# Attention scores in 64x32 array tiles with doubled, half-empty states, and another order of the pieces

## The chip, the cores and the metric

The kernel runs on one core of one Trainium2 chip. The metric is the device time of one execution in microseconds (us); the median of three runs counts. A profile is one execution of its own; its times are read against that execution. Engines are called as the profile calls them: PE (matrix engine; PEld is its weight load), DVE (vector), ACT (scalar), POOL (GpSimd), SP (which only issues stores here).

## What is computed

Two steps follow each other: a two-way attention between 512 tokens and 32 states in each of 8 batches and 8 heads, and a dense layer pair over all 4352 rows that come out of it.

```python
def _attn_ref(x, state):              # x (8, 8, 512, 64), state (8, 8, 32, 64)
    scores = scale * np.matmul(x, state.transpose(0, 1, 3, 2))
    ...                               # softmax over the 32 states
    xread = np.matmul(a, state)
    scores2 = scale * np.matmul(state, x.transpose(0, 1, 3, 2))
    ...                               # softmax over the 512 tokens
    sread = np.matmul(a2, x)
    return np.concatenate([xread, sread], axis=2)

def _moe_ref(x, w_in, w_out, s, b):   # d_model 512, d_ff 2048
    r = np.maximum(x @ w_in, 0.0)
    return (s * (r * r) + b) @ w_out
```

## The kernel before, in words

**Pieces and order.** All work is cut into some 700 small pieces, and the list `ORDER` (lines 15 to 76) names them one after the other. A word such as `M.2.3.0` calls one helper (table at lines 712 to 722) with its arguments; a last letter A, V or G says whether ACT, DVE or POOL does it. The list is the order of the instructions *on each engine*: an engine works through its own words in this order and waits only for data and for buffers, so the place of a DVE word between two PE words sets no time by itself. The same holds for DMA issues: loads `x`, `xn`, `win`, `wout` and `st` are issued by POOL and stand in line with POOL's arithmetic, stores by SP (some late ones by ACT).

**Pieces of one batch b** (heads are held as two groups g of four, r is the head in its group):
- `xT` (line 284): DVE transposes 32x32 blocks of x, two 16-bit values e = 0, 1 as a pair. `pair` (253) does the same for the states into `stE`, for the batches of rows i0 to i1.
- `T` (292): scores of all 8 heads against the states, 16 matmuls: for both e, for four output strips hp of 32 rows and both groups g. Weights are a 32x32 block of `stE`, the array tile is (32 r, 32 hp), and the sum over e is made in PSUM (bank g). `keep` copies scores to SBUF for later.
- `U`, `mu`, `D`, `E1`, `z`, `At`, `A` (313 to 359): softmax over the states; `A` is what the dense layer takes. `nm`, `nms`, `E2`, `a2` (364 to 390): softmax over the tokens. `aps`, `a2T` (392, 398) turn it, `V` (401) multiplies it with x, `srd` (421) puts the result away.
- `M` (424): states times one quarter j of w_in, 8 matmuls in array tiles of 64x32, one output strip hp and group g each; `Mc` copies to fp16. So attention's second product and the first dense layer become one: `l` (476) makes 128 rows f of the hidden layer out of `M` and `A` with two matmuls; its ReLU is on ACT (463). `lh` and `sh` are the halves of that for batch 0, `s` (471) squares.
- `L` (499) and `out`: second dense layer for batches 0 to 2. `wsum`, `S`, `P`, `ev`, `put` (530 to 611): the same for batches 3 to 7 with 7 products in place of 8, which needs sums of weights and of activations; a batch has 14 words `P` of 8 matmuls each. `lsr`, `ssr`, `S_sr`, `P_sr`, `ev_sr`: both layers for the state rows, at the end.
- `idle.n` (666): n matmuls on ones, at the start.

**Buffers in PSUM.** `ps_t` and `ps_a` hold one tile of two banks each, and `T`, `M`, `V`, `aps` and others take turns in them (third argument of `M`, second of `T`: 1 is `ps_t`). `ps_h` holds two tiles for `l`, `ps_o` two for `L` and `P`.

**Head and strip.** In `T`, `V` and `M` the strip hp of a head r in group g is r ^ g (lines 298, 409, 429):

```python
r = hp ^ g
mm(part(T[Ns * hp : Ns * hp + Ns], p, g)[:, 0, :],
   stE[32 * r : 32 * r + 32, NG * b + g, :, e],
   part(at[b]["xT"][32 * r : 32 * r + 32, :, :, e], p, g)[:, 0, :],
   ..., tp=(32 * r, Ns * hp))
```

Of the kernel before, what the change touches and what calls it, by code (L numbers as in the profile page):

```python
# [10 lines left out]
FP32 = mybir.dt.float32  # L11
FP16 = mybir.dt.float16
# [12 lines left out]
    "bias",  # L25
# [54 lines left out]
def kernel(  # L80
# [12 lines left out]
    nc = tc.nc  # L93
    AF = mybir.ActivationFunctionType
    ALU = mybir.AluOpType
    AX = mybir.AxisListType

    B, H, S, D = x.shape
    Ns = state.shape[2]
    DM = H * D  # L100
    DF = moe_w_in.shape[1]
    P = 128
    NK = DM // P
    NKF = DF // P
    NG = H // 4
# [55 lines left out]
    stE = konst.tile([P, NR, Ns, 2], FP16, name="stE")  # L161
# [61 lines left out]
    nc.vector.memset(ones32, 1.0)  # L223
    xh_t[0] = xpool.tile([P, NG, NT, D], FP16, name="xh_0", tag="xh")
# [28 lines left out]
    def pair_states(i0, i1):  # L253
        nc.vector.transpose(
            stE[:, i0:i1].rearrange("p i n e -> p (i n e)").bitcast(FP32),
            stn[:, i0:i1].rearrange("p i d -> p (i d)").bitcast(FP32),
        )

# [33 lines left out]
    def at_T(b, own=1, p=None):  # L292

        at[b]["T", p] = T = two_banks(f"T_{b}_{p}", own=own)
        for e in range(2):
            for hp in range(4):
                for g in range(NG):
                    r = hp ^ g
                    mm(
                        part(T[Ns * hp : Ns * hp + Ns], p, g)[:, 0, :],  # L300
                        stE[32 * r : 32 * r + 32, NG * b + g, :, e],
                        part(at[b]["xT"][32 * r : 32 * r + 32, :, :, e], p, g)[:, 0, :],
                        start=(e == 0), stop=(e == 1),
                        tp=(32 * r, Ns * hp),
                    )
# [451 lines left out]
```

## Time and profile before

| What | Value |
|---|---|
| Median of three runs (lowest, highest) | 218.31 us (218.29, 219.01) |
| The profiled execution's own time | 218.81 us |
| Its span, first to last instruction | 217.0 us |
| PE, PEld busy | 207.7 us, 126.5 us |
| DVE, ACT, POOL busy | 169.8 us, 155.2 us, 103.8 us |
| Granted TensorE clock, mean over the span | 1.000 |
| DMA moved | 22.68 MB |

A matmul's duration in the profile reaches from its first column to the end of its writing, so two in a row overlap and their durations add up to more than the time they take. What a row of matmuls takes is read from start to start. A busy share of 96% says that PE nearly always has a matmul under way, not that it streams at its best.

### The profile page before, as it was taken

How to read it: one execution, taken by the hardware profiler on the slowest of the kernel's cores; microseconds unless marked ns; L12 is line 12 of the kernel's file. 1: busy time of each engine (PE TensorE's matmuls, PEld its weight loads, DVE VectorE, ACT ScalarE, POOL GpSimd, SP SyncE). 2: the span in 40 equal slices, each digit the busy share in tenths (PEclk: the TensorE clock that was granted, in tenths of full speed). 3: DMA queues.
4: the chain of work that ended last, by engine and by line, in shares of the span. 5: the costliest groups of instructions: out<-in, count | busy, mean ns of one | idle time of the engine just before them, and what ended most of it. 6: DMA issues, size and time to landing. Idle time of an engine off the chain costs nothing.

```text
span 217.0 us, 4732 instructions
## 1 busy us (share of the span) xinstructions
PE 207.7 (96%) x1920; PEld 126.5 (58%) x1920; DVE 169.8 (78%) x237; ACT 155.2 (72%) x263; POOL 103.8 (48%) x100
## 2 busy tenths in 40 slices
PE   7868999999999999999999999999999999999992
PEld 2334344343444435545677666776667777888881
DVE  2789885989867869985998799979887964785472
ACT  4477987898858678989889899677669766454400
POOL 8229033494579930434254318837455334225330
PEclk9999999999999999999999999999999999999999
DMA  6999992659597252192908850719912600440045
GB/s 149 236 204 202 205 197 40 103 136 127 118 172 125 48 97 51 24 167 55 145 7 134 133 119 3 98 30 146 200 17 59 139 0 3 91 106 0 0 145 148
DMA packets 23657, 22.68 MB, mean 105 GB/s; under 512 B 4436, under 2 KB 17236, under 8 KB 23636
## 3 DMA queue, kind: packets, MB, share of 16 engines
q0 software_dynamic: 16560, 12.26, 39.4%
q1 hardware_dynamic: 5792, 9.18, 17.2%
q10 hardware_dynamic: 1284, 0.95, 1.6%
q8 instruction: 15, 0.25, 0.4%
q14 instruction: 6, 0.05, 0.1%
HBM read 25.72 MB, written 8.91 MB: 160 GB/s over the span
## 4 chain that ended last, share of the span: by engine, by line
PE 88%; DMA 6%; POOL 2%; ACT 1%; issue 0%; DVE 0%; ACTq 0%; POOLq 0%
PE hps L459 24%; PE ops L503 19%; PE opf_X L138 16%; PE opf_W L138 8%; DMA w_out<-in_moe_w_out_dram 6%; PE opf_Y L138 4%; PE mps L138 4%; PE hps_sr L459 3%; PE vps L138 2%; PE aps L138 2%; PE ops_sr_X L138 2%; PE T_None L138 2%; POOL w_in L201 1%; PE ops_sr_W L138 1%; PE hph L138 1%; POOL xh L184 1%
## 5 line engine op out<-in xcount | busy, mean ns | idle before, releaser
L463 ACT ACTIVATE r<-hps 128x512 f16<-128x512 f32 x120 | 67.5, 602 | 27.8 <-PE hps L459 27.0
L459 PE MATMUL hps<-A,M 128*128 128x512 f16 x240 | 64.8, 380 | 0.0
L138 PEld LDWEIGHTS <-g 128*128 128x128 f16 x480 | 46.6, 98 | 11.4 <-issue 0.7
L503 PE MATMUL ops<-w_out,g 128*128 128x512 f16 x192 | 46.3, 379 | 0.2 <-DMA w_out<-in_moe_w_out_dram 0.2
L469 POOL TENSOR_TENSOR g<-r 128x1024 f16<-128x1024 f16 (+1 forms) x14 | 30.4, 2182 | 24.3 <-ACT r L463 24.3
L459 PEld LDWEIGHTS <-M 128*128 128x128 f16 x240 | 21.7, 98 | 22.8 <-issue 6.4
L503 PEld LDWEIGHTS <-g 128*128 128x128 f16 x192 | 18.7, 98 | 22.5 <-issue 0.8
L153 ACT CAST M<-mps 128x1024 f16<-128x1024 f32 x22 | 22.3, 1017 | 1.6 <-PE mps L138 1.6
L467 ACT ACTIVATE g<-r 128x1024 f16<-128x1024 f16 (+1 forms) x18 | 21.4, 1210 | 0.1
L193 POOL DMA_DIRECT2D xn<-in_x_dram x32 | 18.6, 595 | 5.7 <-PE vps L138 4.9
L344 POOL TENSOR_TENSOR At<-E,rz 128x1024 f16<-128x1024 f16 x5 | 9.8, 1964 | 22.0 <-ACT r L463 11.4
L138 PE MATMUL opf_X<-w_T,g 128*128 128x256 f16 x160 | 19.8, 273 | 0.0
L573 DVE TENSOR_TENSOR g<-g 128x1024 f16<-128x1024 f16 (+1 forms) x20 | 17.9, 908 | 1.1 <-POOL S L573 0.9
L573 POOL TENSOR_TENSOR g<-g 128x1024 f16<-128x1024 f16 x4 | 8.8, 2206 | 19.6 <-PE opf_X L138 12.4
L469 DVE TENSOR_TENSOR g<-r 128x1024 f16<-128x1024 f16 (+1 forms) x18 | 14.7, 837 | 1.6 <-ACT r L463 1.6
L153 DVE CAST M<-mps 128x1024 f16<-128x1024 f32 x10 | 12.1, 1213 | 3.6 <-PE mps L138 3.0
L602 DVE SCALAR_TENSOR_TENSOR osx<-opf_X,sb_bc,bias_bc 128x512 f32<-128x512 f32 x15 | 11.2, 747 | 4.0 <-PE opf_X L138 3.9
L290 DVE STREAM_TRANSPOSE xT<-xh 128x1024 f32<-128x1024 f32 (+2 forms) x12 | 10.4, 874 | 4.4 <-ACT xh L153 3.9
L323 POOL TENSOR_TENSOR Dm<-U,mu 128x1024 f32<-128x1024 f32 x3 | 5.7, 1912 | 14.8 <-DVE mu L319 14.8
L463 ACT ACTIVATE r_sr<-hps_sr 128x256 f16<-128x256 f32 x16 | 6.1, 381 | 7.9 <-PE hps_sr L459 7.2
L138 PE MATMUL mps<-w_in,stT 64*32 64x512 f16 x256 | 11.3, 383 | 0.5 <-DMA w_in<-in_moe_w_in_dram 0.3
L513 DVE SCALAR_TENSOR_TENSOR osb<-ops,sb_bc,bias_bc 128x512 f32<-128x512 f32 x12 | 8.8, 736 | 3.4 <-PE ops L503 3.4
(101 smaller groups left out, 324.8 us busy)
## 6 DMA issues: line engine op xcount, KB each, us to landing
out_dram<-osx SPq DMA_DIRECT2D x36, 128.0 KB, 2.4
xn<-in_x_dram POOLq DMA_DIRECT2D x32, 128.0 KB, 5.3
xh<-in_x_dram POOLq DMA_DIRECT2D x14, 256.0 KB, 4.8
w_in<-in_moe_w_in_dram POOLq DMA_DIRECT2D x8, 256.0 KB, 9.9
w_out<-in_moe_w_out_dram POOLq DMA_DIRECT2D x4, 512.0 KB, 11.3
out_dram<-osb SPq DMA_DIRECT2D x16, 128.0 KB, 3.3
xf<-in_x_dram SPq DMA_DIRECT2D x4, 256.0 KB, 5.2
out_dram<-osb SPq DMA_DIRECT2D x16, 64.0 KB, 4.4
```

The costliest lines, as they stand in the source:

```text
L138: return nc.tensor.matmul(out, lhsT, rhs, start=start, stop=stop, tile_position=tp, is_transpose=is_transpose, skip_group_check=skip,)
L153: (engine.copy if engine is nc.scalar else engine.tensor_copy)(out, in_)
L193: nc.gpsimd.dma_start(out=xn_t[b][32 * jh : 32 * jh + 32].rearrange("t h c d -> t h (c d)"), in_=x[b].rearrange("h (t jh c) d -> jh t h (c ...
L290: nc.vector.transpose(part(out, p, g), part(in_, p, g))
L344: e.tensor_tensor(out, E1, over_n(rz), ALU.mult)
L459: nc.tensor.matmul(hps, lhsT, rhs, start=(i == 0), stop=(i == len(terms) - 1))
L463: nc.scalar.activation(R_t[tag, q][:, i], hps, AF.Relu)
L467: nc.scalar.activation(g, r, AF.Square)
L469: e.tensor_mul(g, r, r)
L503: nc.tensor.matmul(ops_t[tag, rr], G_t[tag][:, f, P * rr : P * rr + P], w_out_f(f), start=(f == 0), stop=(f == NKF - 1),)
L573: e.tensor_tensor(out, x, y, op)
L602: nc.vector.scalar_tensor_tensor(out, fast(b, name[0]), s_bc, out if plus else bias, ALU.mult, ALU.add)
```

## The change

Three things are changed together.
1. **States are stored twice.** `stE` becomes `stZ[0]` and `stZ[1]`. `pair` transposes as before into `stZ[0]`; then two DVE multiplications by the columns of a mask `own` (1 for the rows of heads of one parity, 0 for the other) leave in `stZ[k]` only heads with r % 2 = k, the other head's 32 rows being zero. `own` is made at the start by five small memsets.
2. **`T` works in tiles of 64 rows.** Each of its 16 matmuls takes the 64 rows of a pair of heads; the wrong head meets zero weights. The array tile is (64 (r // 2), 32 hp). Strip and head are now paired by r = hp ^ 2g in `T`, `V` and `M`; the tile of `M` stays (64 g, 32 hp). Counts, columns and accumulation are as before.
3. **All pieces stand in a new order**, and some change their engine or are cut otherwise (a square of 4 rows in place of two of 2, a sum in halves). The three `idle` words go from 12, 12 and 5 matmuls to 11, 10 and 3. Every other PE word occurs in both lists.

```diff
-    stE = konst.tile([P, NR, Ns, 2], FP16, name="stE")
+    stZ = [konst.tile([P, NR, Ns, 2], FP16, name=f"stZ_{k}") for k in range(2)]
+    own = konst.tile([P, 2], FP32, name="own")
...
     nc.vector.memset(ones32, 1.0)
+    nc.vector.memset(own, 0.0)
+    for r in range(4):
+        nc.vector.memset(own[Ns * r : Ns * r + Ns, r % 2 : r % 2 + 1], 1.0)
...
     def pair_states(i0, i1):
         nc.vector.transpose(
-            stE[:, i0:i1].rearrange("p i n e -> p (i n e)").bitcast(FP32),
+            stZ[0][:, i0:i1].rearrange("p i n e -> p (i n e)").bitcast(FP32),
             stn[:, i0:i1].rearrange("p i d -> p (i d)").bitcast(FP32),
         )
+        for k in (1, 0):
+            nc.vector.tensor_scalar(stZ[k][:, i0:i1], stZ[0][:, i0:i1], own[:, k : k + 1], None, ALU.mult)
...
-                    r = hp ^ g
+                    r = hp ^ 2 * g
+                    rows = slice(64 * (r // 2), 64 * (r // 2) + 64)
                     mm(
                         part(T[Ns * hp : Ns * hp + Ns], p, g)[:, 0, :],
-                        stE[32 * r : 32 * r + 32, NG * b + g, :, e],
-                        part(at[b]["xT"][32 * r : 32 * r + 32, :, :, e], p, g)[:, 0, :],
+                        stZ[r % 2][rows, NG * b + g, :, e],
+                        part(at[b]["xT"][rows, :, :, e], p, g)[:, 0, :],
                         start=(e == 0), stop=(e == 1),
-                        tp=(32 * r, Ns * hp),
+                        tp=(64 * (r // 2), Ns * hp),
                     )
...
-                    hp = k ^ g
+                    hp = k ^ 2 * g
...
-                r = hp ^ g
+                r = hp ^ 2 * g
```

The start of the list, then the stretch around the piece `V.5.2`, then the end:

```diff
-    "castx.1.0.A xT.0.1.0 casts.A idle.12 pair.0.4 castx.0.0.A xT.0.0.0 T.0.1.0 U.0.0 turn.0.4.A mu.0.0 "
-    "D.0.V.0 E1.0.0 sb idle.12 castx.1.1.V keep.0.0 xT.0.1.1 castx.0.1.A win.0 M.1.0.0 M.0.0.1 x.1 z.0.0 "
-    "xT.0.0.1 At.0.V.0 A.0.0 win.1 wout.0 T.0.0.1 U.0.1 Mc.1.0.A mu.0.1 D.0.V.1 Mc.0.0.A lh.0.2.0 xT.1.1 "
-    "lh.0.0.0 keep.0.1 xT.1.0 idle.5 E1.0.1 win.2 M.0.1.0 T.1.1 sh.0.0.0.V Mc.0.1.A z.0.1 At.0.V.1 A.0.1 "
-    "lh.0.6.0 lh.0.4.0 keep.1 sh.0.6.0.V sh.0.4.0.V sh.0.2.0.G L.0.1.0 lh.0.0.1 lh.0.4.1 lh.0.2.1 M.0.2.0 "
-    "Mc.0.2.A lh.0.6.1 L.0.0.0 win.3 l.0.8 l.0.10 M.1.2.1 Mc.1.2.A M.0.3.0 U.1 mu.1 D.1.V l.0.11 "
-    "sh.0.2.1.V wout.1 l.0.9 M.1.1.1 wout.2 Mc.0.3.V wout.3 sh.0.0.1.V M.1.3.0 E1.1 l.0.13 l.0.12 st "
-    "s.0.10.2.V L.0.0.1 L.0.1.1 z.1 Mc.1.3.A x.2 s.0.12.2.A l.0.15 At.1.V s.0.8.2.G L.0.1.2 l.0.14 A.1 "
+    "win.0 win.1 castx.1.0.A xT.0.1.0 x.1 castx.0.0.A casts.A idle.11 xT.0.0.0 turn.0.4.A castx.1.1.A "
+    "wout.0 pair.0.4 T.0.1.0 U.0.0 mu.0.0 D.0.V.0 sb E1.0.0 xT.0.1.1 castx.0.1.A z.0.0 At.0.V.0 xT.0.0.1 "
+    "keep.0.0 idle.10 M.1.0.0 Mc.1.0.A M.0.0.1 Mc.0.0.A A.0.0 T.0.0.1 U.0.1 keep.0.1 mu.0.1 lh.0.2.0 "
+    "lh.0.0.0 D.0.V.1 E1.0.1 xT.1.0 M.0.1.0 idle.3 win.2 xT.1.1 Mc.0.1.A T.1.1 win.3 keep.1 z.0.1 "
+    "At.0.V.1 sh.0.0.0.G sh.0.2.0.G lh.0.4.0 lh.0.6.0 sh.0.4.0.G L.0.1.0 A.0.1 lh.0.2.1 lh.0.4.1 lh.0.0.1 "
+    "M.0.2.1 U.1 wout.1 Mc.0.2.A lh.0.6.1 wout.2 st sh.0.6.0.V L.0.0.0 l.0.8 sh.0.4.1.G l.0.10 M.0.3.1 "
+    "sh.0.2.1.V M.1.2.0 Mc.1.2.A l.0.11 l.0.9 mu.1 D.1.V E1.1 M.1.1.1 sh.0.6.1.G sh.0.0.1.G Mc.0.3.V "
+    "M.1.3.0 l.0.14 L.0.0.1 s.0.10.2.V l.0.15 Mc.1.3.A L.0.1.1 s.0.8.2.V l.0.12 z.1 At.1.V wout.3 "
+    "Mc.1.1.A l.0.13 L.0.0.2 A.1 L.0.1.2 l.1.11 s.0.14.2.V l.1.2 cps.0 cps.1 pair.4.16 cps.2 cps.3 c "
...
+    "nm.6 nms.6.A wsum.T2.1.G ev.3.Y P.3.5 l.4.13 aps.2 xn.2 ev.3.X2 S.3.4.2.G l.4.8 P.3.6 U.6 mu.6 nm.0 "
+    "P.3.8 a2T.2.V wsum.T4.1.G P.3.7 ev.3.W1 E2.6.0 P.3.9 ev.3.X3 E2.6.1 s.4.12.4.A M.6.0.1 s.4.6.2.A "
+    "V.5.2 srd.2 srd.5 a2.6 s.4.4.2.A S.4.3.0.V l.4.10 S.4.1.0.V nms.0.V P.3.10 wsum.T4.0.G P.3.12 P.3.11 "
...
-    "P.7.8 P.7.9 ssr.6.2.A S_sr.3.0.V ssr.14.2.A ssr.10.2.A P_sr.0 ev.7.X3 S_sr.1.2.G P.7.10 S_sr.2.0.V "
-    "S_sr.3.1.V P.7.11 ev_sr.0.0.X.0.0 P.7.12 P.7.13 put.6.1.0 put.6.1.1 ev.7.W2 put.7.0.0 S_sr.2.1.V "
-    "ev.7.X4 P_sr.1 P_sr.2 P_sr.3 ev_sr.0.1.X.0.0 P_sr.4 ev_sr.1.1.W.0.0 put.7.0.1 put.7.1.0 S_sr.4.2.G "
-    "ev_sr.0.0.Y.1.1 put.7.1.1 ev_sr.1.1.X.1.1 P_sr.5 P_sr.6 ev_sr.0.1.W.1.1 ev_sr.1.0.X.0.1",
+    "ev.7.X3 lsr.13 ssr.8.2.V lsr.12 P.7.10 ssr.12.2.V P.7.12 S_sr.1.1.V S_sr.3.2.V S_sr.2.0.V P.7.13 "
+    "ev.7.X4 P_sr.0 P.7.11 put.6.1.0 P_sr.1 ev_sr.0.0.X.0.0 S_sr.4.0.G S_sr.2.1.G P_sr.2 P_sr.3 ev.7.W2 "
+    "ev_sr.0.1.X.0.0 put.6.1.1 put.7.0.0 P_sr.4 S_sr.4.1.G ev_sr.1.1.W.0.0 P_sr.5 put.7.0.1 put.7.1.0 "
+    "put.7.1.1 ev_sr.1.1.X.1.1 P_sr.6 ev_sr.0.0.Y.1.1 ev_sr.0.1.W.1.1 ev_sr.1.0.X.0.1",
```

How the tiled PE words stand side by side (a row of them with no other PE word between is called a cluster here, a part of a cluster in one tile shape a segment; before, `T` and `M` differ in shape, after they don't), from `L.0.1.0` on:

| | clusters | segments | `T` beside `M` in one cluster | `V` beside `M` |
|---|---|---|---|---|
| before | 23 | 29 | T.2/M.2.3, T.3/M.2.0, T.5/M.3.3, T.6/M.5.1 | V.3.4/M.5.0, V.6.0/M.6.3 |
| after | 22 | 25 | none of two shapes; in one shape: T.2/M.2.3, T.3/M.2.0, T.5/M.3.3, T.6/M.5.1, T.7/M.6.1 | V.3.4/M.5.0, V.5.2/M.6.0, V.6.0/M.6.3 |

More of the change, by code (lines that the diff above doesn't have):

```diff
@@ L15 @@
 ORDER = [
[9 rows of a table removed]
-    "bias",
[50 rows of a table removed]
[58 rows of a table added]
 ]
```

89 rows, old and new, of the table ORDER are left out of this document.

## Prediction

> **What bounds the kernel now.** I read the page's busy shares first, then its slices, then the table by stretches of time, then PE's timeline from start to start.
>
> ```profile
> PE 207.7 (96%) x1920; PEld 126.5 (58%) x1920; DVE 169.8 (78%) x237; ACT 155.2 (72%) x263; POOL 103.8 (48%) x100
> ...
> PE   7868999999999999999999999999999999999992
> ```
>
> PE is busy in every slice but those at the two ends. The table by stretches (PE, PEld, DVE, ACT, POOL busy in each) sharpens it:
>
> ```profile
> 60.00:100.00 40.00, 40.00 (x336) 17.83 (x335) 32.11 (x42) 31.98 (x55) 20.86 (x17) 1.00 0.54 93
> 100.00:140.00 40.00, 40.00 (x419) 27.81 (x417) 35.71 (x50) 34.70 (x57) 20.85 (x21) 1.00 0.59 93
> 140.00:180.00 40.00, 40.00 (x405) 28.55 (x405) 32.72 (x48) 29.48 (x52) 19.45 (x16) 1.00 0.46 81
> ```
>
> PE has 40.00 of 40.00 us at full clock, DVE at most 35.7, ACT 34.7. Busy can hide slow rows, so I take steps from PE's timeline:
>
> ```profile
> 18.78 1.02 PE L503 MATMUL ops<-w_out,g 128*128 128x512 f16 x4 [0.22 <-DMA w_out<-in_moe_w_out_dram]
> 19.64 1.04 PE L138 MATMUL hph<-A,M 128*128 128x256 f16 x8
> 20.99 0.60 PE L138 MATMUL hph<-A,M 128*128 128x256 f16 x4 [0.31 <-ACT rh L489]
> ...
> 24.20 0.63 PE L138 MATMUL mps<-w_in,stT 64*32 64x512 f16 x16
> 24.76 1.04 PE L459 MATMUL hps<-A,M 128*128 128x512 f16 x4
> ...
> 37.98 0.60 PE L459 MATMUL hps<-A,M 128*128 128x512 f16 x2
> 38.51 0.64 PE L138 MATMUL T_None<-xT,stE 32*32 32x512 f16 x16
> 39.08 0.41 PE L138 MATMUL mps<-w_in,stT 64*32 64x512 f16 x8
> 39.42 0.60 PE L459 MATMUL hps<-A,M 128*128 128x512 f16 x2
> ```
>
> Four `ops` take 0.86 (18.78 to 19.64), so a word `l` 0.43 and `L` 0.86; elsewhere a word `P` takes 0.87. Two `M` together take 0.56 (24.20 to 24.76), one alone 0.34 (39.08 to 39.42): 0.22 each plus 0.12 once. The two `hps` ahead of `T` take 0.53 instead of 0.43: entering a tiled cluster costs 0.10. `T` takes 0.57 (38.51 to 39.08): 0.45 plus the same 0.12, paid although `M`, tiled too, comes next. So a cluster costs 0.10, and each segment in one tile shape 0.12.
>
> With these steps I add up PE from `L.0.1.0` at 18.78: 120 `l` 51.8, 48 `L` 41.4, 70 `P` 61.1, state rows 13.1, four `lh` 1.7, aps 3.6, `V` 4.1, six `T` 2.7, 29 `M` 6.4, the few others 1.5, 29 segments 3.5, 23 clusters 2.3: 193.2. PE really needs 194.1 (18.78 to 212.8); 0.9 is stall, nearly all before 27 us. From there PE streams to the end, and the tail (212.8 to 217.0) is one eviction and a store. **The bound is PE's own stream from 18.78 on, and 18.78 is when w_out.0 lands.**
>
> **The change, part by part.**
>
> *T in 64x32.* Counts and columns stay. Eight of its matmuls run at once before (16 of 512 columns in 0.45, as 16 of `M` in 64x32 take 0.44), and eight distinct tiles remain, so `T` costs 0.45 after too. Gained are segments: `T` beside `M` no longer changes shape. By the table of clusters, 29 segments become 25 and 23 clusters 22: 4 x 0.12 + 0.10 = **-0.58**. Bounds: 0 if the 0.12 is paid between any two kinds of tiled work, -0.58 if it is the shape's; I take -0.58, since two `M` in a row pay it once.
>
> [...]
>
> *States twice.* `pair` adds two multiplications. The nearest row is DVE's TENSOR_SCALAR of 128x512 f16 by a column, 364 ns. For 128x256 I take 0.2 each (bounds 0.1 to 0.36), for 128x768 0.5 (0.36 to 0.73). The five memsets (the row of 1x128 has 165 ns) make 0.8 in DVE's 3.05 us of waiting for the first xh: hidden. The first `pair` lies ahead of `T.0.1.0` and now behind castx.0.0 as well: `T.0.1.0` about 0.9 later than 6.12. Its chain made A.0.0 ready at 12.6, while `lh.0.2.0` waits for Mc.0.0 until 13.7, because of w_in.0; the cover is 1.1, the cost nothing, 0.2 if both multiplications take the upper bound. The second `pair` falls where DVE stood idle 1.19 and 1.28 us around `c` and `bias`: nothing, and if that cover is gone `T.2.1` waits for xT.2 by up to 1.0.
>
> *Start.* POOL now issues win.1 ahead of x.1; the 2 MB up to w_out.0 are the same, so it lands at 18.8 again. x.1 lands where win.1 did, near 15.9, and xT.1 begins at 15.4 in halves: `T.1.1` perhaps 0.2 later, under the wait for w_out.0 (0.22 of it is left). Likewise the dummies (29 to 24) all lie ahead of that wait: nothing. Both half squares that `L.0.1.0` needs are POOL's now, not one (1.30 each; 0.38 on DVE): from rh.0.0.0 at about 15.8 to 18.4, in time by 0.4. keep.1 now stands ahead of two ReLUs on ACT, and I find `lh.0.0.1` waiting about as long as `lh.0.2.1` did. Stalls there: same, within 0.7.
>
> *The other moves.* Over the whole list, with a duration for each kind from its row, ACT loses 1.3 us, POOL 2.8, and DVE gains 1.5 beside the masks. None becomes the bound over a stretch, so only single deadlines count. Three are tight. (1) `V.5.2`: from P.3.5's end PE has 5.25 until it; DVE needs ev 0.72, U, mu, nm 3 x 1.25 with gaps, a2T.2 0.69, hand-offs 0.2: 5.36, 0.1 late. (2) The end: from lsr.12 to P_sr.2 six words, 5.24; ReLU 0.6, squares and sums on DVE 0.42 + 0.42 + 0.69 + 0.42, two halves on POOL 1.19 each, hand-offs 0.3: 5.23, just in time. (3) P.3.0 needs out.2.3, 0.75 after L.2.3.3, and has 0.95. I allow **+0.15** for all (bounds 0 and 1.0).
>
> *Sum.* -0.58 + 0.15 = -0.43. The profiled execution took 218.81, 217.0 of it span: 216.6 + 1.81 = 218.4 by it. The median shown is 0.50 lower, 218.31, and goes to **217.9**.
>
> **The rivals.**
>
> A, the sum: 217.9, chance 0.56, by itself 217.2 to 218.7.
>
> B, slower: **w_out.1 comes late.** POOL's line shows where it stands before:
>
> ```profile
> 9.94 0.61 POOL L201 DMA_DIRECT2D w_in<-in_moe_w_in_dram  x1 [3.55 <-DMA w_in<-in_moe_w_in_dram]
> 15.03 1.30 POOL L469 TENSOR_TENSOR g<-rh 128x512 f16<-128x512 f16 x1 [4.47 <-ACT rh L489]
> 16.28 1.27 POOL L201 DMA_DIRECT2D w_in<-in_moe_w_in_dram  x2
> 17.54 2.27 POOL L207 DMA_DIRECT2D w_out<-in_moe_w_out_dram  x3
> ```
>
> The ninth load (9.94) waits until the first has landed; after, win.3 follows it at once and waits for the next landings, to about 13, ahead of POOL's squares. w_out.1 was issued at 17.54. After, it stands behind sh.0.4.0.G, which waits for a ReLU at about 19.05: issue at 20.35. `L.0.0.1` wants it at 27.1. The four loads of w_out took 8.6 to 13.8 to land; at 8.6 from the issue it lands at 29.0, and PE stands 1.9: 219.8. It decides from a landing over 6.75 after the issue. Against it: loads land in the order of issue at some 0.5 MB per 2.5 us (w_in.0 11.2, w_out.0 18.8, the states 32.5), and what lies ahead is no more than before, so the bytes, not the issue, set about 26.2. Chance 0.15.
>
> C, the change does not do what it says: the 0.12 stays between `T` and `M`. Only 0.10 for the cluster is left, and V.5.2 beside M.6.0 saves nothing: 218.4. Against it the row of two `M`. Chance 0.10.
>
> D, slower: **two row tiles on one bank.** After, tiles of rows 0 and 64 both write bank g of `T`, in other strips; in `M` each row tile has a bank of its own. Were they to take turns, each of six `T` would take 0.45 more: 220.6. Against it: before, four row tiles (32 r for r = 0 to 3) write one bank, and `T` keeps the pace of `M`. Chance 0.04.
>
> [...]
>
> E, faster: **the stalls of the start go.** 0.9 lies before 27 us, all of it ReLU or `Mc` wait; if the new order of ACT clears 0.7: 217.2. For it: POOL takes four half squares off DVE, and `Mc.1.1` leaves DVE. Against it: the producers ahead of each wait are the same. Chance 0.15.
>
> **How the numbers follow.** A measurement tells about 0.5% from no change: 217.2 and 219.4 are the marks. Faster: most of E (0.11) and A's lower end (0.13): 0.24. Slower: B (0.12), D (0.04), A's upper end, two of the tight deadlines missed at once (0.01): 0.17. Same: 0.59. For the range, A with C and E reach from 216.9 (E with no tight deadline missed) to 218.7, B to 219.8; outside stay D and the ends, under 0.2.
>
> **What would show it.** In PE's timeline: `T` then `M` in one cluster 0.45 + 0.34 from start to start (right), 0.57 + 0.34 (C), 0.9 for `T` (D). The first `ops` at 18.8 and the second group of `ops` for q = 1 near 27, with no wait for w_out (B if there is one). The step sum from `L.0.1.0`: 192.6 and a stall total below 1.2. V.5.2 waiting for DVE a2T, P_sr.2 for POOL: at most 0.2 each. Wrong I would be above all if many small waits of 0.1 to 0.3 stand in the stretches 100 to 180, where DVE is fullest, or if w_out.0 itself lands at another time than 18.8: every 0.1 of that goes straight into the result.

## The result, and the profile after

The changed kernel takes **224.08 us** (median of six executions, 223.11 to 225.94) against 218.30 for the kernel before beside it: a ratio of 1.026, interval 1.0235 to 1.0294. The forecast was 217.9, with 219.8 as its upper end.

The profiled execution took 223.11 us with a span of 221.2. On its page PE's busy line reads much as before (209.1 us, 95%); the slices show where it does not: a 7 and an 8 in the middle of PE's row (about 127 to 138 us), and a 7 in the row of the granted clock.

```profile
PE 209.1 (95%) x1915; PEld 126.0 (57%) x1915; DVE 176.8 (80%) x248; ACT 154.9 (70%) x261; POOL 101.5 (46%) x102
...
PE   7869999999999999999999978999999999999992
...
PEclk9979999999999999999999999999999999999999
```

The table by stretches (PE, PEld, DVE, ACT, POOL busy, then clock, DMA share, GB/s) puts it at 120 to 140. Before, PE had 20.00 there and the DMA engines were 0.54 busy.

```profile
100.00:120.00 20.00, 20.00 (x246) 13.60 (x245) 17.14 (x25) 15.77 (x26) 16.43 (x10) 1.00 0.33 55
120.00:140.00 20.00, 18.16 (x174) 12.71 (x172) 15.18 (x26) 14.40 (x25) 8.14 (x13) 1.00 0.76 133
```

PE's timeline, with the rows that answer to those of before (first column start, second duration):

```profile
18.55 1.03 PE L508 MATMUL ops<-w_out,g 128*128 128x512 f16 x4
19.64 1.05 PE L136 MATMUL hph<-A,M 128*128 128x256 f16 x8
...
27.47 1.02 PE L508 MATMUL ops<-w_out,g 128*128 128x512 f16 x4 [0.26 <-DMA w_out<-in_moe_w_out_dram]
...
39.38 0.65 PE L136 MATMUL T_None<-xT,stZ 64*32 64x512 f16 x16
39.84 0.40 PE L136 MATMUL mps<-w_in,stT 64*32 64x512 f16 x8
40.17 0.61 PE L464 MATMUL hps<-A,M 128*128 128x512 f16 x2
...
130.52 1.04 PE L464 MATMUL hps<-A,M 128*128 128x512 f16 x4
133.40 1.91 PE L136 MATMUL opf_X<-w_T,g 128*128 128x256 f16 x16 [1.84 <-DVE osx L607]
```

`T` then `M` take 0.46 and 0.33 from start to start: the tiles do what was forecast. But `T.2.1` starts at 39.38 and not at 38.51, and at 130.52 four `hps` of 0.86 are followed by the next row only 2.88 later. The row that PE waits for is DVE's `ev.4.X1`, and that one waits for a store:

```profile
128.22 1.22 DVE L578 TENSOR_TENSOR g<-g 128x2048 f16<-128x2048 f16 x1
132.59 0.75 DVE L607 SCALAR_TENSOR_TENSOR osx<-opf_X,sb_bc,bias_bc 128x512 f32<-128x512 f32 x1 [3.15 <-DMA out_dram<-osx]
...
153.70 0.75 DVE L607 SCALAR_TENSOR_TENSOR osx<-opf_X,sb_bc,bias_bc 128x512 f32<-128x512 f32 x1 [1.14 <-DMA out_dram<-osx]
```

`osx` has one buffer for each half of a batch's rows, so `ev.4.X1` may write only when the four stores of this half of batch 3 are done. SP issues them from 123.45 on. Before, the last eviction into this half (`ev.3.W2`) and the `ev.4.X1` that follows stood further apart, and neither waited:

```profile
120.83 0.74 DVE L602 SCALAR_TENSOR_TENSOR osx<-opf_W,sb_bc,osx 128x512 f32<-128x512 f32 x1
...
129.22 0.75 DVE L602 SCALAR_TENSOR_TENSOR osx<-opf_X,sb_bc,bias_bc 128x512 f32<-128x512 f32 x1
```

POOL's timeline of the changed kernel shows what is issued beside the stores, and the DMA view of 118 to 132 what that does (last column: median us from issue to landing):

```profile
120.47 1.16 POOL L183 DMA_DIRECT2D xh<-in_x_dram  x2
121.61 4.04 POOL L192 DMA_DIRECT2D xn<-in_x_dram  x7
125.81 0.58 POOL L192 DMA_DIRECT2D xn<-in_x_dram  x1 [0.15 <-issue]
```

```profile
xn<-in_x_dram POOLq DMA_DIRECT2D x8, 128.0 KB, 7.7
out_dram<-osx SPq DMA_DIRECT2D x8, 128.0 KB, 7.1
```

The same view of the kernel before:

```profile
out_dram<-osx SPq DMA_DIRECT2D x8, 128.0 KB, 2.4
```

`x.7`, `xn.6` and `xn.0` stand one behind the other on POOL in the new list. Before, POOL issued them at 112.4, 116.3 and 134.3.

**The account**, from the start of `L.0.1.0` to the start of `P_sr.6`: 197.55 against 193.17, +4.38. Against the steps that the prediction used, waits ahead of `T.2.1` are 2.04 in place of 0.72 (+1.32), the store wait is 2.02, a second one 0.89 (`ev.5.X1` at 153.70; the sum `S.5.1.1` on POOL comes late through it, `D.7` stands right behind it there, and a DVE sum beside `D.7` takes 2.38; PE stalls at 158.8 to 161.3), two late rows behind `V.7.1` 0.42, and the tiles give -0.58: 4.07 together. The other 0.31 lies in smaller differences, 0.21 of it ahead of `T.2.1`, where the whole difference is 1.53 (20.83 against 19.73, and the old list has one word `l` of 0.43 more there).

### The profile page after: what moved, and what is told of

The parts are those of the page before. It is cut to its first block, busy times and chain, and to the rows that moved or that the text cites. A ratio compares the mean times of both kernels' runs of the same rounds, so it can differ in the third digit from the quotient of the medians.

```text
span 221.2 us, 4735 instructions
## 1 busy us (share of the span) xinstructions
PE 209.1 (95%) x1915; PEld 126.0 (57%) x1915; DVE 176.8 (80%) x248; ACT 154.9 (70%) x261; POOL 101.5 (46%) x102
## 4 chain that ended last, share of the span: by engine, by line
PE 64%; DMA 11%; DVE 9%; ACT 5%; POOL 4%; issue 2%; SPq 2%; DVEq 0%; POOLq 0%
PE ops L508 16%; PE hps L464 16%; PE opf_X L136 10%; DMA out_dram<-osx 5%; PE opf_W L136 4%; DMA w_out<-in_moe_w_out_dram 4%; PE hps_sr L464 3%; PE mps L136 3%; PE opf_Y L136 2%; DVE osx L607 2%; DVE g L578 2%; DMA xf<-in_x_dram 2%; SPq L616 2%; POOL g L474 2%; PE ops_sr_X L136 2%
## 5 line engine op out<-in xcount | busy, mean ns | idle before, releaser
L468 ACT ACTIVATE r<-hps 128x512 f16<-128x512 f32 x120 | 68.4, 605 | 29.4 <-PE hps L464 28.0
L349 POOL TENSOR_TENSOR At<-E,rz 128x1024 f16<-128x1024 f16 x6 | 12.3, 2043 | 36.3 <-DVE rz L340 23.9
L474 DVE TENSOR_TENSOR g<-r 128x1024 f16<-128x1024 f16 (+1 forms) x22 | 20.5, 945 | 7.3 <-ACT r L468 7.3
L472 ACT ACTIVATE g<-r 128x1024 f16<-128x1024 f16 (+1 forms) x18 | 22.7, 1265 | 0.2
L474 POOL TENSOR_TENSOR g<-r 128x1024 f16<-128x1024 f16 (+1 forms) x7 | 14.9, 2139 | 13.6 <-ACT r L468 13.5
L578 DVE TENSOR_TENSOR g<-g 128x1024 f16<-128x1024 f16 (+1 forms) x20 | 19.1, 957 | 0.9 <-POOL g L578 0.5
L578 POOL TENSOR_TENSOR g<-g 128x1024 f16<-128x1024 f16 (+1 forms) x4 | 10.5, 2619 | 14.2 <-DVE S L578 5.5
L151 DVE CAST M<-mps 128x1024 f16<-128x1024 f32 x9 | 10.8, 1212 | 1.0 <-PE mps L136 1.0
L637 POOL TENSOR_TENSOR g_sr<-g_sr 128x512 f16<-128x512 f16 x3 | 3.4, 1155 | 15.8 <-DVE g_sr L637 15.7
L136 PE MATMUL opf_Y<-w_out,g 128*128 128x256 f16 x80 | 10.2, 273 | 0.0
```

The costliest lines, as they stand in the source:

```text
L136: return nc.tensor.matmul(out, lhsT, rhs, start=start, stop=stop, tile_position=tp, is_transpose=is_transpose, skip_group_check=skip,)
L151: (engine.copy if engine is nc.scalar else engine.tensor_copy)(out, in_)
L349: e.tensor_tensor(out, E1, over_n(rz), ALU.mult)
L468: nc.scalar.activation(R_t[tag, q][:, i], hps, AF.Relu)
L472: nc.scalar.activation(g, r, AF.Square)
L474: e.tensor_mul(g, r, r)
```

## The experiments

The theory after these traces: **(S)** the order costs the time, by putting loads beside stores that a single buffer must wait for. Rivals: the doubled states and their masks cost it; the stores are late for another reason; the start costs it; a lower clock costs it.

### The tiles without the order

The changed code with the list of before.

> The changed kernel's code (states twice, T in 64x32) with the order of before. If the order is at fault and the tiles do what the step sum says: 218.3 - 4 x 0.12 us for the shape changes that go (T beside M in four clusters), so 217.8, T then M 0.45 + 0.34 from start to start, no new stall. If the tiles or the doubled states are at fault: near 224.

Measured: 219.17 (ratio 1.0032, 1.0011 to 1.0054). Each `T` beside an `M` is 0.12 shorter, yet the kernel does not gain. DVE's timeline shows the masks (the two multiplications at L263) between `stZ` and `xT`, and PE's the wait:

```profile
36.70 0.57 DVE L258 STREAM_TRANSPOSE stZ<-stn 128x384 f32<-128x384 f32 x1
37.30 0.88 DVE L263 TENSOR_SCALAR stZ<-stZ,own 128x768 f16<-128x768 f16 x2
38.09 1.24 DVE L296 STREAM_TRANSPOSE xT<-xh 128x1024 f32<-128x1024 f32 x1
```

```profile
39.38 0.65 PE L138 MATMUL T_None<-xT,stZ 64*32 64x512 f16 x16 [0.52 <-DVE xT L296]
```

So in PE's steps the masks eat what the tiles save, about 0.5 against 0.5, because of where `pair.4.16` stands. The expected 217.8 was missed by more than that: the median is 0.70 above the kernel before beside it. In the profile 0.29 of this is a later `L.0.1.0` (19.07 against 18.78), and 0.36 lies behind it (193.53 against 193.17).

### The order without the tiles

The code of before with the new list.

> The code of before (32x32, states once) with the new order. If the order is at fault: 224.1 plus the 0.6 that the tiles save, 224 to 225, with the same waits: DVE for a store near 132 and near 153, PE for w_out near 27 and 34. If the tiles are at fault: near 218.

Measured: 224.72 (1.028, 1.024 to 1.032), with `ev.4.X1` waiting 3.17 for the same stores. **The order alone makes the loss**; the masks are out as its cause.

### Two buffers for the first output tile

```diff
-t = opool.tile(..., tag=f"osx{key}", bufs=1)
+t = opool.tile(..., tag=f"osx{key}", bufs=2 - int(key))
```

Room for it comes from one buffer less for `osb` (4 to 3) and one shared by `stf` and `c16`.

> The changed kernel, with a second buffer for output tile 0 of batches 3 to 7 (room for it comes from one buffer less for the outputs of batches 0 to 2 and from letting two small tiles share a place), so that the first eviction of a batch no longer waits for the stores of the one before. If those store waits make up the middle part of the loss: PE's 1.84 before P.4.4 and the 0.54 near 160 go, 224.1 falls by 2.5 to 3.5 to 220.6 to 221.6. If the eviction would be late for another reason (DVE's own backlog): by less than 1.

Measured: 219.75 (1.0046, 1.0027 to 1.0065). Both waits are gone, though the stores still take 6.9 us to land. PE's rows at the place of the first:

```profile
129.10 1.04 PE L464 MATMUL hps<-A,M 128*128 128x512 f16 x4
129.97 1.91 PE L136 MATMUL opf_X<-w_T,g 128*128 128x256 f16 x16
```

**Without the wait, 4.3 of the 5.8 us are gone**, more than the 2.5 to 3.5 that were expected. Not all of it is the wait itself. In the two profiles (223.11 and 218.78) PE's stalls behind the stores make 2.91; another 1.41 lies ahead of `T.2.1` (39.38 against 37.97), where no store is waited for, and where the clock was halved from 13.30 to 16.70 in the one profile and full in the other. That the clock makes this 1.41 is argued, not shown.

### Loads moved away from the stores, with one buffer

First `x.7` alone, to ahead of `S.3.4.2.G`:

> The changed kernel with one load, x.7, moved in POOL's queue to ahead of S.3.4.2 (issued some 10 us sooner), so that only xn.6 and xn.0 are under way when batch 3 is stored. If the loads that share the DMA engines make the stores slow: stores of 128 KB that took 7 us near 125 take 4 to 6, the wait of ev.4.X1 falls from 3.1 to 1 to 2, the time by 1 to 2, to 222 to 223. If the stores are slow by themselves (number, order on their queue): no change.

Measured: 222.35. The stores still took 6.5 us and `ev.4.X1` waited 2.86, so the wait hardly fell: the eight loads of `xn.6` and `xn.0` are enough. That the time came out in the expected 222 to 223 is luck: it fell by 1.73, the wait by 0.29 only. Two of the four executions had a mean clock of 1.00; of the six of the changed kernel none had (0.982 to 0.996). Then these too:

> The changed kernel, still with one buffer for the first output tile, but with its loads of x taken apart: x.7 goes ahead of S.3.4.2.G, xn.6 goes to where V.5.2 gives its buffer free (behind srd.5), and xn.0 goes behind At.6.G. So no load is issued just ahead of the stores of batch 3. Theory (the eight row loads in one go are what makes those stores land in 7 us): the stores land in 2.5 to 4 us, the wait of ev.4.X1 falls from 2.9 (with x.7 moved alone) to below 0.8, PE's stall there from 1.7 to below 0.3, and the time from 222.35 to 220.3 to 221.0, since the second wait (ev.5.X1) and the stalls of the start stay. Rival (the stores are slow because they are issued late and in long runs by SP, whatever the loads do): the wait stays above 2 us and the time at 222.0 to 222.7.

Measured: 223.66 (1.0254, 1.0195 to 1.0313), 2.7 more than the theory allowed, and yet its mechanism is in the trace: the stores land in 2.4 us and no eviction waits for them. The loss is a new wait that this edit made itself. `xn.6` needs a buffer that `V.5.2` frees, and `wsum.T4.0` stands behind it on POOL:

```profile
113.86 2.13 POOL L548 TENSOR_TENSOR w_T<-w_out,w_T 128x1024 f16<-128x1024 f16 x1
118.44 2.35 POOL L192 DMA_DIRECT2D xn<-in_x_dram  x4 [2.45 <-PE vps L136]
120.81 2.13 POOL L548 TENSOR_TENSOR w_T<-w_out,w_T 128x1024 f16<-128x1024 f16 x1
```

```profile
122.99 1.03 PE L136 MATMUL opf_X<-w_T,g 128*128 128x256 f16 x8 [2.93 <-POOL w_T L548]
```

With `xn.6` behind that sum, and `xn.7` taken from the stores of batch 4 as well:

> The changed kernel, still with one buffer for the first output tile, and its loads kept clear of the stores without a new wait on POOL: x.7 ahead of S.3.4.2.G, xn.6 behind wsum.T4.0.G (in the run with xn.6 behind srd.5, POOL stood 2.45 us for V.5.2 there, with wsum.T4.0.G queued behind it, and PE stalled 2.93), xn.0 behind At.6.G, and xn.7 behind S.5.1.1.G, so that it is clear of the stores of batch 4 too. Theory (loads crowd the stores, and this alone makes ev.4.X1 and ev.5.X1 wait): the stores of both batches land in 2.4 to 4 us, each of the two waits is below 0.5, and the time is that of the kernel with two buffers, 219.0 to 220.2. Rival (one buffer is too little even then, because ev.4.X1 comes 6.0 us behind the last eviction of batch 3 instead of 7.6): a wait of 1 us or more stays, and 220.5 to 222.

Measured: 220.97 (1.0102, 1.0067 to 1.0138). Stores of both batches land in 2.4, and no eviction waits for one; the time lies in the range of the rival, but the wait that the rival named is not there. PE stalls 1.37 behind 157.50, a new stall again made by this edit: `D.7` on POOL now stands behind the issues of `xn.7`, and runs from 155.68.

```profile
157.50 1.03 PE L464 MATMUL hps<-A,M 128*128 128x512 f16 x4
159.73 1.91 PE L136 MATMUL opf_W<-w_out,g 128*128 128x256 f16 x16 [1.21 <-DVE osx L607]
```

So `xn.7` goes one word later on POOL (`S.5.1.1`, called a square in what follows, is a sum):

> The kernel with its loads kept clear of the stores and one buffer (220.97 median), with xn.7 one word later on POOL, behind D.7.G instead of ahead of it. In that run D.7 started 2.47 us behind S.5.1.1 and not 0.1, ACT's E1.7 waited 0.73 for it with two ReLUs queued behind, and PE stalled 1.37 at 157.50. Theory (this stall is only the xn.7 issues ahead of D.7; the stores no longer cost anything): no stall there, no wait of ev.4.X1 or ev.5.X1 above 0.3, and 1.1 to 1.5 less, 219.4 to 219.9, which is the time with two buffers (219.75). Rival (the stall at 157.50 is the late square S.5.1.1 on POOL, which stays where it is): 220.6 to 221.2 again.

Measured: **219.76** (1.0044, 1.0023 to 1.0066), the 219.75 of the two buffers; the stall is gone. The way by `E1.7` and the ReLUs on ACT is not the one in the trace, though: PE's row at 159.73 waited for DVE's `ev.5.W1`, which stood behind a sum of 128x2048 that took 2.82 beside `D.7` in the one run; with `xn.7` later it takes 1.22, since `D.7` then runs beside the sum ahead of it (1.80). One buffer is enough: `ev.4.X1` starts 4.8 us behind the end of the last eviction into this half (124.28) and does not wait, since the last of the four stores landed at 128.57; in the changed kernel it stood ready after 6.0 us and waited 3.15 more.

```profile
123.53 0.75 DVE L607 SCALAR_TENSOR_TENSOR osx<-opf_W,sb_bc,osx 128x512 f32<-128x512 f32 x1
...
129.12 0.74 DVE L607 SCALAR_TENSOR_TENSOR osx<-opf_X,sb_bc,bias_bc 128x512 f32<-128x512 f32 x1
```

### The same fault put into the kernel before

Two words of the old list moved, `xn.6` and `xn.0` behind `S.4.3.0.G`:

> The kernel before, with nothing changed but two words of its order: xn.6 and xn.0 both go behind S.4.3.0.G, so that POOL issues their eight row loads in one go from about 122.4, beside the stores of batch 3 (issued from 121.6). Theory: these stores land in 5 to 8 us instead of 2.4; ev.4.X1 comes 7.6 us behind the last eviction of batch 3 there, so it waits 0.3 to 1.7 us for them, and the time rises from 218.4 to 218.7 to 220.0. Rival (the load burst is harmless, the slowness of the stores comes from something else in the new order): 2.4 us to land, no wait, 218.2 to 218.6.

Measured: 219.76 against 218.79 beside it (1.0043, 1.0010 to 1.0076). The stores, which landed in 2.4, now take 5.9, and an eviction that never waited waits (DVE's timeline, then the DMA view of 118 to 132):

```profile
131.14 0.75 DVE L602 SCALAR_TENSOR_TENSOR osx<-opf_X,sb_bc,bias_bc 128x512 f32<-128x512 f32 x1 [1.23 <-DMA out_dram<-osx]
```

```profile
out_dram<-osx SPq DMA_DIRECT2D x8, 128.0 KB, 5.9
xn<-in_x_dram POOLq DMA_DIRECT2D x8, 128.0 KB, 7.1
```

The first two stores, issued ahead of the loads (122.20 and 122.78, the loads from 122.96 on), still landed in 2.4; the next two took 4.9 and 6.9. With the fault taken out of one kernel and put into the other, (S) is shown: loads beside the stores make the wait. How much of the loss is the wait stands under the run with two buffers.

### The start and the clock

What is left with two buffers is 1.3 us. In the changed kernel's profile the clock is halved for 3.4 us, just behind a stretch in which PE was busy for half of the time (columns as in the table by stretches):

```profile
9.90:13.30 3.40, 1.69 (x35) 0.42 (x33) 2.99 (x7) 3.16 (x5) 1.22 (x2) 1.00 1.19 208
...
13.30:16.70 3.40, 3.09 (x26) 1.45 (x19) 3.33 (x6) 2.58 (x6) 0.45 (x1) 0.50 1.20 206
```

Eight `hph` take 1.82 there from start to start (13.64 to 15.46); at 17.67, where the clock is full, 0.88. By an estimate from this stretch (half of 3.4, of 221), one such stretch brings the mean clock of an execution to 0.992. With two buffers 8 of 10 executions were at 0.992 or below; of the kernel before, 2 of 94 beside all these runs. So dummies were put into the gaps of PE (on top of two buffers):

> The changed kernel with two buffers for the first output tile (219.75 median), and with three dummy products more ahead of M.0.0.1 and three ahead of T.0.0.1, where PE stood idle 0.87 and 0.69 us. The dummies compute nothing that is used. Theory (short idle stretches of PE in the first 13 us bring a stretch of half clock of some 3.4 us, which costs about 1 us): the granted clock is 1.0 (0.996 or more) in nearly all executions instead of 0.992 in most, and the median falls by 0.7 to 1.1, to 218.6 to 219.1. Rival (the clock falls for another reason, such as the load of all engines): the clock stays at 0.992 in most executions and the time at 219.5 to 219.9, or up to 0.3 longer if a dummy is in the way.

> The changed kernel with two buffers for the first output tile, two dummies more ahead of M.0.0.1 and three ahead of T.0.0.1, keep.0.0 ahead of castx.0.1 on ACT, and srd.1 behind s.7.8.2 instead of right behind srd.7. Theory (what is left over the step sum is the wait of M.0.0.1 for keep.0.0 and the two reads of the state rows back to back on ACT): 0.3 to 0.5 less than with the dummies alone, since the 0.14 and 0.27 behind V.7.1 go and the start gains up to 0.3: 218.1 to 218.6, about the kernel before. Rival (the start is set by another chain, and the ReLUs are late anyway): the same as with the dummies alone, within 0.2.

Measured: 219.67 and 219.63. The first half of the theory held in part: 4 and 2 of 12 executions are still at 0.992 or below. The second failed: the medians did not fall. Within the first of these runs, executions at 0.992 or below average 220.28 and the others 219.43, 0.85 apart; in the second they are 0.43 apart, with two buffers alone 0.40 (two executions against eight), and in the last run with one buffer 0.16, where the 8 of 12 executions above 0.992 still average 219.60. So in these runs the halved clock is not most of the 1.3 us. In the profile of the first run with dummies `L.0.1.0` starts at 19.37 and not 17.93; in that of the second it starts at 18.04, but PE then waits 0.41 and 0.29 around the second and last load of w_out. Moving `srd.1` did not remove the late rows behind `V.7.1` either (0.39 in one place instead of 0.14 and 0.27). How the 1.3 us divide stays open.

### The tiles with the masks in a gap

The run of the tiles alone, with one word moved:

```diff
-cps.3 Mc.1.1.V l.1.10 s.1.10.2.G l.1.6 L.0.0.3 c bias l.1.0 l.1.5 pair.4.16 xT.2
+cps.3 Mc.1.1.V l.1.10 s.1.10.2.G l.1.6 L.0.0.3 pair.4.16 c bias l.1.0 l.1.5 xT.2
```

> The change of the tiles alone, in the order of before (219.17 median), with pair.4.16 moved from behind bias to ahead of c, where DVE stood idle 1.19 us. Theory (the 0.52 us that T.2.1 waited for xT.2 is the masks' time, and with the masks in that gap the saving of the tiles comes through): T.2.1 waits 0.1 at most, T then M take 0.46 and 0.34, and the time falls by 0.5, to 218.5 to 218.8, with the late start (0.29) as the remainder. Rival (the states land too late, near 34 us, so that pair there holds c up and with it bias and cps): the wait moves to bps and PE keeps 0.4 or more of it: 219.0 to 219.6.

Measured: 218.30 (0.9989, 0.9965 to 1.0013), and once more:

> The tiles of the change in the order of before with pair.4.16 ahead of c, once more, to narrow its interval (218.30 against 218.42, ratio 0.9989 with 0.9965 to 1.0013). Theory (four of the segments of 0.12 go, and nothing else changes from L.0.1.0 on): 0.3 to 0.5 less than before, 217.9 to 218.2. Rival (the masks ahead of T.0.1.0 delay the start by as much in most executions): no difference, 218.3 to 218.6.

Measured: **217.82** against 218.79 (0.9951, 0.9928 to 0.9974). The states had landed in time (`pair` starts at 32.05, right behind `Mc.1.1`; in the first of the two profiles it waited 0.27 for them), `T.2.1` waits for nothing, and from `L.0.1.0` to `P_sr.6` PE needs 192.83 and 192.70 in the two profiles, 0.34 and 0.47 less than before. The gains by the medians, 0.12 and 0.97, lie on both sides of that, and the medians of the kernel before beside them differ by 0.37; the traces bear out 0.3 to 0.5. This version has the lowest median of all here.

## Why the prediction was wrong, point by point

**"None becomes the bound over a stretch, so only single deadlines count. Three are tight"**: this step failed. Only deadlines between arithmetic pieces were searched. `V.5.2`, `P_sr.2` and `P.3.0` held without a stall, but the deadline that mattered was that of a buffer: the stores of batch 3 against `ev.4.X1`. It was not in the list, nor among the rivals, because in the profile of before no eviction waits for a store. The margin was in that profile all the same: the last eviction into this half of batch 3 ended at 121.57, SP issued its four stores one after the other from 121.60 to 123.46, the last of them landed at 125.93, and `ev.4.X1` began at 129.22, 3.3 us later. The new list both cut the time between the two evictions from 7.6 to 6.0 us and put 1.5 MB of loads beside the stores, the last of which landed at 132.47. The term of "+0.15, bounds 0 and 1.0" measured 2.9 in PE's rows; without the wait the median fell by 4.3.

**"Start ... same, within 0.7"**: wrong by about as much again. Stalls between `L.0.1.0` and `T.2.1` are 2.04, not 0.72. In the profile with two buffers, at full clock, `T.2.1` comes 20.04 behind `L.0.1.0` and not 20.83, so 0.79 of the 1.53 does not recur there. That `L.0.1.0` came at 18.55, near the forecast 18.8, is luck: by the trace w_out.0 landed at 17.85, and PE did not wait for it; the rows ahead ran at half clock. With two buffers and full clock `L.0.1.0` came at 17.93.

**Rival B** happened in small: w_out.1 was issued at 20.38 (20.35 was worked out) and PE waited 0.26 for it, not 1.9, so the landing was about 7 us behind the issue and not 8.6. The last load of w_out, which stands behind three half squares, cost another 0.34, and this was not looked at.

**Tiles, -0.58**: right in the steps. In the old list, where four segments go (0.48), the two profiles gave 0.34 and 0.47; the 0.58 of the new list was not measured by itself. **C** (the 0.12 stays between `T` and `M`) and **D** are refuted by the 0.46 and 0.33 above. No run shows the 0.45 more for each `T` that D's 220.6 takes: `T` takes 0.46 with rows 0 and 64 on one bank in other strips.

**States twice**: the price of the second `pair` if its cover is gone was put at "up to 1.0"; without the new order it was 0.52. In the new order the cover holds, as forecast. The duration was right in size: 0.88 for the two of 128x768, against 1.0 taken.

**Clock**: taken as 1.00, and no rival touched it. Five of the six executions of the changed kernel were at 0.992 or below, two of them (0.982 and 0.983, 224.54 and 225.94 us) about what two such stretches make by the estimate above (0.985). What one costs is not settled: 0.16 to 0.85 between executions of one kernel.

## What to carry to other kernels

In a list that fixes the order of every engine, a load is not just an issue on its queue: ask which stores it will fly beside (2.4 us to land became 5.9 to 7.1 here), and how long before the buffer of these stores is written again. A buffer for which nobody waits still has a margin, and it can be read from the profile of before: from the last write of the old contents to the first of the new, less the time until the last of its stores has landed. Here that is 4.4 us for four stores issued in a row, not the 2.4 of one. And a load holds up whatever stands behind it on its engine, while it waits for its buffer (2.45 us, a stall of PE of 2.93) and while its four issues take their 2.3 us (a stall of 1.37), as two of the mends here showed.

## What was not expected of the hardware

- Stores of 128 KB that land in 2.4 us in the kernel before took longer when eight loads of 128 KB were issued beside them: 5.9 with the two words moved in the kernel before, 6.5 with `x.7` moved, and with two loads of 256 KB as well 6.9 (two buffers) and 7.1 (the changed kernel). The traces show only the landing times, not what makes them longer.
- Some sums on DVE took far longer beside work of POOL. In the run with `xn.6` behind `srd.5`, one of 128x1024, which takes 0.69 alone, took 4.48 beside a sum and `D.6` of POOL (120.81 to 124.80) and ended 0.56 behind them:

```profile
120.88 4.48 DVE L578 TENSOR_TENSOR S<-g 128x1024 f16<-128x1024 f16 x1 [1.36 <-ACT g L472]
```

  Such sums also carried the late `D.7` on to PE in the changed kernel (2.38 beside `D.7`; PE at 158.8 to 161.3) and with `xn.7` ahead of it (2.82 and not 1.22; PE at 157.50). Why they take longer no trace shows.
- The clock fell to half for 3.4 us behind short waits of PE, but not behind all of them. In the run of the order alone it did so in the middle of the kernel, right behind the store wait, and 16 `opf_X` took 3.16 and not 1.75:

```profile
130.00:133.80 3.80, 1.94 (x24) 0.74 (x23) 1.02 (x2) 2.78 (x5) 0.00 (x0) 1.00 1.22 301
133.80:137.20 3.40, 3.40 (x18) 2.27 (x16) 3.37 (x6) 0.00 (x0) 0.15 (x1) 0.50 0.65 95
```

  In the 3.40 us ahead PE was busy for 1.54 there (130.4 to 133.8), and for 1.69 ahead of the stretch at the start of the changed kernel's profile (9.90 to 13.30). But the wait of 1.84 us in the changed kernel's profile left the clock at 1.00, with PE busy for 1.56 of the 3.40 us ahead (130.0 to 133.4), and so did the waits at the start with two buffers, with 1.53 of 3.40 (9.9 to 13.3, the clock at 1.00 from 13.3 to 16.7). In the run with `xn.6` behind `srd.5` PE waited 2.93, and the clock stood at 1.00 from 120 to 140. So PE's busy time ahead does not tell by itself when the clock falls; that stays open.
